# Attention and gated MLP in split fp32: P times V of a head pair in one group instead of two, and narrower score matmuls

## The chip, the cores and the metric

The kernel runs on one core of a Trainium2 chip. The metric is device time in microseconds; three runs of the kernel before gave a median of 1383.16 us (1382.53 to 1386.95).

## The reference

Block-causal attention over 8 batches, 8 heads, 576 positions of 64 dimensions, and then a two-layer MLP with a rational activation:

```python
scores = scale * np.matmul(q, k.transpose(0, 1, 3, 2))
mask = block_i >= block_j                 # blocks of 64 positions
scores = np.where(mask, scores, -1000000000.0)
attn = softmax(scores)                    # with the row maximum taken off, 1e-9 added to the sum
x = concat_heads(np.matmul(attn, v))      # (4608, 512)
h = x @ w_in                              # (4608, 2048)
g = (a0 + a1*h + a2*h**2 + a3*h**3) / (1 + |b0|*|h| + |b1|*h**2 + 1e-6)
out = g @ w_out                           # (4608, 512)
```

## The kernel before

**Number format.** Every operand of a large matmul is held as a high and a low part of type F32R, whose sum is the fp32 value. A product is three matmuls: high by low, high by high, low by high. Transposes on TensorE (PE) are in plain fp32.

**Attention.** The 64 heads are handled as 32 pairs, one pair after the other (NV = 32; four pairs to a batch). The 576 query rows of a pair are five tiles t: 64 rows, then four times 128 (NQ, starting at Q0). Tile t needs the first NK[t] keys: 64, 192, 320, 448, 576. For a tile and one head j, `scores` issues two matmuls (L432, L433) that give S for 128 rows and at least 256 columns, and, but for t = 0, a third (L436) that adds the mask to the last 64 columns; VectorE (DVE) takes the row maximum (L437). `expo` does the exponential on ScalarE (ACT, L449) and the normalization on GpSimd (POOL, L458, L462). `transp` turns P of both heads into blocks of 128 keys by up to 128 queries (L481); each group of blocks in one PSUM bank is copied by ACT to the high part (L486) and subtracted by DVE to the low part (L487). There are 1 + 2t blocks for tile t.

**P times V.** `pv` runs twice per pair. Group 0 follows tile 2 and covers the 320 query columns of tiles 0 to 2: block 0 over 320 columns from the tiles `pt0`, blocks 1 to 4 over 256 columns from `pt1`, whose part that tile 1 doesn't have is zero. Group 1 follows tile 4 and covers the 256 columns of tiles 3 and 4: nine blocks from `pt2`. V stands in `vpad`, two heads side by side; `vprep` fills it for the next pair after group 1. The result (PSUM tile `o`) is split into `x` by ACT (L503) and DVE (L504) and written to a DRAM scratch `xscr`, one DMA for each group (L505).

**MLP.** Its unit of work is 2 x 128 hidden columns by 256 tokens in phase 0 (18 chunks c of 5 units u, the first 10 hidden blocks) and 128 by 512 in phase 1 (the other 6 blocks). `first` does 24 matmuls (L207), then ACT, POOL and DVE compute the activation (L214 to L240), and `second` does 12 matmuls of 512 columns (L257). Phase 0 is threaded through the attention from the fifth pair on; what is left of it and phase 1 follow after the attention. While the attention runs, `split_weights` also splits the weights (L122 to L149).

**What sets the order.** The program is written out as a list of steps: the item of tile t and head j of a pair is one step, ten steps to a pair; `transp` of a tile comes nine steps after its scores, `pv` one step after that. A scheduler then reorders each engine's instructions by a simulated timeline, so neighbouring work moves when an instruction changes. Each engine takes its instructions strictly in that order; SP issues the DMAs.

**Buffers.** Scores, transposed P and `o` share a ring of five PSUM banks (`ps_a`, tag "a"). `pt0`, `pt1`, `pt2` and `vpad` exist once, so the next pair may overwrite a block only after P times V has read it.

Of the kernel before, what the change touches and what calls it, by code (L numbers as in the profile page):

```python
# [9 lines left out]
F32 = mybir.dt.float32  # L10
# [51 lines left out]
def attn_ffn_kernel(  # L62
# [11 lines left out]
    nc = tc.nc  # L74
# [231 lines left out]
    NK = [64, 192, 320, 448, 576]  # L306

    wpool = ctx.enter_context(tc.tile_pool(name="wA", bufs=1))
    with ExitStack() as actx:
# [5 lines left out]
        pt0 = [apers.tile([128, 1, 320], F32R, name=f"pt0{x}") for x in "hl"]  # L315
        pt1 = [apers.tile([128, 4, 256], F32R, name=f"pt1{x}") for x in "hl"]
        pt2 = [apers.tile([128, 9, 256], F32R, name=f"pt2{x}") for x in "hl"]

        vpad = [apers.tile([128, 128 + 4 * 192], F32R, name=f"vp{x}") for x in "hl"]
        for x in pt1:  # L320
            nc.vector.memset(x[:, 2:4, 0:128].bitcast(F32), 0.0)
        for x in pt2:
            nc.vector.memset(x[:, 7:9, 0:128].bitcast(F32), 0.0)
# [90 lines left out]
        def scores(p, t, j):  # L414
# [13 lines left out]
            for i, (c0, w) in enumerate(pieces(t)):  # L428
                ww = max(w, 256)
                ps = ps_a.tile([128, 512], F32, name=f"s{p}_{t}_{j}_{i}", tag="a")  # L430
                last = t > 0 and c0 + w == NK[t]
                nc.tensor.matmul(ps[:, :ww], lhsT=kq[:, 0, qs], rhs=kq[:, 1, c0:c0 + ww], start=True, stop=False)  # L432
                nc.tensor.matmul(ps[:, :ww], lhsT=kq[:, 0, qs], rhs=kq[:, 2, c0:c0 + ww],  # L433
                                 start=False, stop=not last)
                if last:
                    nc.tensor.matmul(ps[:, w - 64:w], lhsT=mrow, rhs=mcol, start=False, stop=True)  # L436
                nc.vector.reduce_max(out=nm[:nq, j, i:i + 1], in_=ps[:nq, :w], axis=AX.X, negate=True)  # L437
                banks.append(ps)
# [27 lines left out]
        def transp(p, t):  # L466
# [3 lines left out]
            groups = {1: [1], 3: [1, 2], 5: [1, 4], 7: [4, 3], 9: [3, 3, 3]}[nb]  # L470
            blk = 0
            for gi, gn in enumerate(groups):
                ps = bank(p, f"t{p}_{t}_{gi}").rearrange("p (c t) -> p c t", c=4)
                for i in range(gn):
# [3 lines left out]
                    else:  # L478
# [3 lines left out]
                (hi, lo), b0, c0 = ((pt2, blk, Q0[t] - 320) if t > 2 else (pt0, 0, Q0[t]) if blk == 0 else  # L482
                                    (pt1, blk - 1, Q0[t] - 64))
                dh = hi[:, b0:b0 + gn, c0:c0 + nq]
                dl = lo[:, b0:b0 + gn, c0:c0 + nq]
# [4 lines left out]
        def pv(p, g):  # L490
            b, hp = divmod(visits[p][0], NPAIR)
            vh, vl = vpad
            nb, w = ((5, 320), (9, 256))[g]
            o = ps_a.tile([128, 512], F32, name=f"o{p}_{g}", tag="a")
            for x in range(nb):
                s0 = 64 if (g == 0 and x > 0) else 0
                hi, lo = ((y[:, x] for y in pt2) if g else (y[:, 0] for y in pt0) if x == 0 else
                          (y[:, x - 1] for y in pt1))
                for i, (vv, pp) in enumerate(((vh, lo), (vh, hi), (vl, hi))):
                    nc.tensor.matmul(o[:, s0:w], lhsT=vblock(vv, x), rhs=pp,  # L500
                                     start=(x == 0 and i == 0), stop=(x == nb - 1 and i == 2))
            xs = att.tile([128, 2, 320], F32R, name=f"x{p}_{g}", tag="xs", bufs=1)
            nc.scalar.copy(out=xs[:, 0, :w], in_=o[:, :w])  # L503
            nc.vector.tensor_tensor(out=xs[:, 1, :w], in0=o[:, :w], in1=xs[:, 0, :w].bitcast(F32), op=ALU.subtract)  # L504
            nc.sync.dma_start(out=xscr[b][:, hp, :, g * 320:g * 320 + w], in_=xs[:, :, :w].bitcast(F32))  # L505
# [7 lines left out]
        def attn_steps():  # L513
# [8 lines left out]
            for k in range(len(items) + ALAG2 + ALAG3 + 8):  # L522
# [3 lines left out]
                if k < len(items):  # L526
# [9 lines left out]
                    if j == 1:  # L536
                        lag = min(ALAG3, nxt[k] - 1)
                        at(k + lag, transp, p, t)
                        if t in (2, 4):
                            at(k + lag + 1, pv, p, t // 4)  # L540
                            if t == ts[-1] and p + 1 < NV:
# [90 lines left out]
```

## Time and profile before

| | |
|---|---|
| median of three runs | 1383.16 us |
| the profiled execution, span from first to last instruction | 1379.1 us |
| PE busy | 1278.1 us, 93% of the span |
| DVE, POOL, ACT busy | 1027.2, 958.2, 909.4 us |
| attention ends (last DMA of `x`) | 980.6 us |

The profile page holds no time for the profiled execution but its span; the median of the runs is 4.1 us above that span, and all sums below are differences made against the span. In a timeline row of PE the first number is the start and the second the modelled duration of the matmul, which overlaps the next one; the distance from one start to the next is what a matmul costs in a stream. PEld is the weight load that goes with each matmul.

### The profile page before, as it was taken

To read this page: it belongs to the slowest core of one execution; us is meant where nothing else is said; L and a number is where in the kernel's file an instruction comes from. 1 tells how busy PE (TensorE), PEld (TensorE's weight loads), DVE (VectorE), ACT (ScalarE), POOL (GpSimd) and SP (SyncE) were. 2 spreads that over 40 slices of the span, in tenths; PEclk is the share of its full clock that TensorE was granted. 3 is DMA by queue.
4 is the path that set the end of the run, shared out by engine and by line. 5 is a ranking of instruction groups with operands and counts; after the bars stand their busy time and mean duration, and the time that the engine had idled before them with its cause. 6 is when DMAs were issued, how large, how long until landed. Compare 5 with 4: busy or idle time off the path is not lost.

```text
span 1379.1 us, 24416 instructions
## 1 busy us (share of the span) xinstructions
PE 1278.1 (93%) x8088; PEld 1149.6 (83%) x8088; DVE 1027.2 (74%) x2048; ACT 909.4 (66%) x2250; POOL 958.2 (69%) x1240
## 2 busy tenths in 40 slices
PE   4677899999899979999999999999989999999997
PEld 3667788999888879888998999998979888888885
DVE  5898877787778857887767777776676767676675
ACT  4766767777677756777767777776645655555553
POOL 4889987687678747777767676666556666666654
PEclk9788999999999999999999999999999999999999
DMA  9778556666556655665654555652632233333332
GB/s 216 198 196 238 146 150 166 168 166 181 148 145 150 164 151 132 165 166 153 157 140 123 154 134 122 160 127 65 213 141 77 77 123 123 122 123 123 122 113 86
DMA packets 216925, 200.84 MB, mean 146 GB/s; under 512 B 129504, under 2 KB 184800, under 8 KB 216800
## 3 DMA queue, kind: packets, MB, share of 16 engines
q1 hardware_dynamic: 216736, 199.28, 53.6%
q8 instruction: 65, 1.06, 0.3%
q14 instruction: 60, 0.49, 0.1%
q0 software_dynamic: 64, 0.00, 0.0%
HBM read 98.57 MB, written 44.04 MB: 103 GB/s over the span
## 4 chain that ended last, share of the span: by engine, by line
PE 69%; DVE 9%; POOL 9%; DMA 5%; ACT 3%; issue 3%; SPq 1%; POOLq 0%; DVEq 0%; ACTq 0%
PE h L207 25%; PE o L257 24%; PE o L500 8%; PE t L481 4%; PE s L432 3%; PE s L433 2%; PE tp L366 2%; POOL gl L240 1%; POOL p L462 1%; DMA x<-xscr 1%; POOL u L217 1%; DVE v L231 1%; DVE nm L437 1%; POOL v L216 1%; DMA xscr<-x 1%
## 5 line engine op out<-in xcount | busy, mean ns | idle before, releaser
L207 PE MATMUL h<-x,wih 128*128 128x256 f32 (+1 forms) x1872 | 415.7, 313 | 9.0 <-DMA x<-xscr 7.9
L207 PEld LDWEIGHTS h<-x,wih 128*128 128x128 f32 x1872 | 309.7, 191 | 29.1 <-issue 6.6
L207 PE MATMUL h<-x,wil 128*128 128x256 f32 (+1 forms) x936 | 290.7, 311 | 0.0
L240 POOL TENSOR_TENSOR gl<-s,gh 128x512 fp32r<-128x512 f32 x144 | 188.8, 1313 | 106.4 <-ACT gh L239 103.0
L257 PE MATMUL o<-woh,gl 128*128 128x512 f32 x576 | 232.2, 403 | 12.1 <-POOL gl L240 10.6
L257 PE MATMUL o<-wol,gh 128*128 128x512 f32 x576 | 227.7, 396 | 0.0
L257 PE MATMUL o<-woh,gh 128*128 128x512 f32 x576 | 227.7, 395 | 0.0
L437 DVE TENSOR_REDUCE nm<-s 128x1 f32<-128x288 f32 (+4 forms) x384 | 161.7, 427 | 78.4 <-PE s L436 45.2
L449 ACT ACTIVATE p<-s,nm 128x288 f32<-128x288 f32 (+4 forms) x384 | 184.9, 485 | 48.3 <-DVE nm L437 35.0
L217 POOL TENSOR_TENSOR u<-v,u 128x512 f32<-128x512 f32 x144 | 189.6, 1317 | 9.8
L216 POOL TENSOR_SCALAR v<-u,bab 128x512 f32<-128x512 f32 x144 | 118.9, 826 | 98.1 <-ACT u L214 94.6
L207 PEld LDWEIGHTS h<-x,wil 128*128 128x128 f32 x936 | 178.7, 191 | 8.7
L462 POOL TENSOR_SCALAR p<-p,rc 128x128 f32<-128x128 f32 (+3 forms) x256 | 164.8, 655 | 29.6 <-DVE rc L457 27.7
L218 DVE TENSOR_TENSOR s<-s,h 128x512 f32<-128x512 f32 x144 | 98.5, 684 | 100.1 <-ACT s L215 99.4
L432 PE MATMUL s<-kq 128*128 128x256 f32 (+3 forms) x384 | 137.3, 360 | 24.3 <-DMA kq<-hl 8.9
L224 ACT ACTIVATE v<-u,qcb 128x512 f32<-128x512 f32 x144 | 104.6, 726 | 69.6 <-POOL u L217 68.9
L214 ACT ACTIVATE u<-h 128x512 f32<-128x512 f32 x144 | 85.9, 596 | 94.2 <-PE h L207 90.1
L239 ACT CAST gh<-s 128x512 fp32r<-128x512 f32 x144 | 89.2, 623 | 82.1 <-DVE s L232 81.5
L257 PEld LDWEIGHTS o<-woh,gl 128*128 128x128 f32 x576 | 109.2, 190 | 35.5 <-POOL gl L240 14.3
L257 PEld LDWEIGHTS o<-wol,gh 128*128 128x128 f32 x576 | 109.1, 189 | 22.2
L257 PEld LDWEIGHTS o<-woh,gh 128*128 128x128 f32 x576 | 109.3, 190 | 18.9
L433 PE MATMUL s<-kq 128*128 128x256 f32 (+3 forms) x384 | 120.1, 315 | 0.0
(105 smaller groups left out, 3043.5 us busy)
## 6 DMA issues: line engine op xcount, KB each, us to landing
kq<-hl SPq DMA_DIRECT2D x64, 432.0 KB, 4.3
kq<-hl SPq DMA_DIRECT2D x64, 288.0 KB, 5.3
x<-xscr SPq DMA_DIRECT2D x56, 256.0 KB, 4.2
xscr<-x SPq DMA_DIRECT2D x32, 320.0 KB, 4.7
qr<-in_q_dram SPq DMA_DIRECT2D x64, 144.0 KB, 2.9
kr<-in_k_dram SPq DMA_DIRECT2D x64, 144.0 KB, 3.0
kq<-hl SPq DMA_DIRECT2D x64, 144.0 KB, 4.8
pscr<-os SPq DMA_DIRECT2D x18, 512.0 KB, 2.9
```

The costliest lines, as they stand in the source:

```text
L207: nc.tensor.matmul(h[:, j, :], lhsT=w[:, dc, fs], rhs=xs[dc][:, hl, :], start=(dc == 0 and i == 0), stop=(dc == 3 and i == 2))
L216: nc.gpsimd.tensor_scalar(out=vt, in0=ut, scalar1=b1, scalar2=b0, op0=ALU.mult, op1=ALU.add)
L217: nc.gpsimd.tensor_tensor(out=ut, in0=vt, in1=ut, op=ALU.mult)
L224: nc.scalar.activation(out=vt, in_=ut, func=AF.Ln, bias=qcb)
L240: nc.gpsimd.tensor_tensor(out=gl.rearrange("p j t -> p (j t)"), in0=st, in1=gh.rearrange("p j t -> p (j t)").bitcast(F32), op=ALU.subtract)
L257: nc.tensor.matmul(self.o[m], lhsT=g[:, j, ms], rhs=w[:, f, :], start=(u == 0 and j == 0 and i == 0), stop=(u == nu - 1 and j == NBU[ph] - ...
L432: nc.tensor.matmul(ps[:, :ww], lhsT=kq[:, 0, qs], rhs=kq[:, 1, c0:c0 + ww], start=True, stop=False)
L433: nc.tensor.matmul(ps[:, :ww], lhsT=kq[:, 0, qs], rhs=kq[:, 2, c0:c0 + ww], start=False, stop=not last)
L437: nc.vector.reduce_max(out=nm[:nq, j, i:i + 1], in_=ps[:nq, :w], axis=AX.X, negate=True)
L449: nc.scalar.activation(out=pt[:nq, j, c0:c0 + w], in_=banks[i][:nq, :w], func=AF.Exp, bias=nm[:nq, j, 0:1], scale=1.0, accum_out=sm[:nq, j ...
L462: nc.gpsimd.tensor_scalar(out=pt[:nq, jj, 64:n], in0=pt[:nq, jj, 64:n], scalar1=rc[:nq, jj:jj + 1], scalar2=1.0, op0=ALU.mult, op1=ALU.mult)
L500: nc.tensor.matmul(o[:, s0:w], lhsT=vblock(vv, x), rhs=pp, start=(x == 0 and i == 0), stop=(x == nb - 1 and i == 2))
```

## The change

P times V becomes one group per pair, issued after tile 4, over 64 columns (tile 0) and 512 columns (tiles 1 to 4). All transposed P of a pair lives in one tile pair `ptr` of 30 blocks of 128 columns: block x of tile t in slot 7(t-1)+x, tile 0 in the first half of slot 12. With that spacing, block x of the tiles c0+1 to 4 is one strided operand (slots 7 apart), and a matmul covers 512, 384, 256 or 128 columns, just those tiles that have the block. The zeroing of `pt1` and `pt2` goes away. The result is split into free slots of the same tile (second half of slot 12, and slots 3 to 6) and written with four DMAs instead of two. Transposes of tile 1 fill one bank instead of two, those of tile 2 go as 3 + 2 instead of 1 + 4. The score matmuls of the tiles 0 and 1 are 64 and 192 columns wide instead of 256.

```diff
-                ww = max(w, 256)
+                ww = w
...
-            groups = {1: [1], 3: [1, 2], 5: [1, 4], 7: [4, 3], 9: [3, 3, 3]}[nb]
+            groups = {1: [1], 3: [3], 5: [3, 2], 7: [4, 3], 9: [3, 3, 3]}[nb]
...
+                b0 = PT0 if t == 0 else 7 * (t - 1) + blk
+                dh, dl = (y[:, b0:b0 + gn, 0:nq] for y in ptr)
...
-        def pv(p, g):
+        def pv(p):
...
+            for i, (vv, pp) in enumerate(((vh, pl), (vh, ph), (vl, ph))):
+                nc.tensor.matmul(o0[:, 0:64], lhsT=vblock(vv, 0), rhs=pp[:, PT0, 0:64],
+                                 start=i == 0, stop=i == 2)
...
+            for x in range(9):
+                c0 = max(0, (x - 1) // 2)
+                for i, (vv, pp) in enumerate(((vh, pl), (vh, ph), (vl, ph))):
+                    nc.tensor.matmul(o1b[:, c0:4, :], lhsT=vblock(vv, x), rhs=pp[:, 7 * c0 + x:22 + x:7, :],
+                                     start=(x == 0 and i == 0), stop=(x == 8 and i == 2))
+            xh0, xl0 = (y[:, PT0, 64:128] for y in ptr)
+            xh1, xl1 = (y[:, 3:7, :].rearrange("p c t -> p (c t)") for y in ptr)
+            for o, xh, xl, q0, w in ((o0, xh0, xl0, 0, 64), (o1, xh1, xl1, 64, 512)):
+                nc.scalar.copy(out=xh, in_=o[:, :w])
+                nc.vector.tensor_tensor(out=xl, in0=o[:, :w], in1=xh.bitcast(F32), op=ALU.subtract)
+                for k, y in enumerate((xh, xl)):
+                    nc.sync.dma_start(out=xscr[b][:, hp, k, q0:q0 + w], in_=y.bitcast(F32))
...
-                        if t in (2, 4):
-                            at(k + lag + 1, pv, p, t // 4)
-                            if t == ts[-1] and p + 1 < NV:
+                        if t == 4:
+                            at(k + lag + 1, pv, p)
+                            if p + 1 < NV:
                                 at(k + lag + 1, vprep, p + 1)
```

Three places in the program show what moves. In the rows, `o12` is P times V of pair 12, `s13_4_0_1` the scores of pair 13, tile 4, head 0, second half, `tp14` the transposes of Q and K of pair 14, `h0_4_0` the first layer of MLP phase 0, chunk 4, unit 0. Line numbers of the changed kernel differ by a few.

PE before, at group 0 of pair 12, half a pair ahead of group 1:

```order
L436 MATMUL s13_2_0_0_5016<-mcol_102,mrow_101 128x64
L500 MATMUL o12_0_5059<-pt0l_129,vph_134 128x320 [waits DVE_49,PE_49,Activation_49]
L500 MATMUL o12_0_5059<-pt0h_128,vph_134 128x320
L500 MATMUL o12_0_5059<-pt0h_128,vpl_135 128x320 [waits Pool_49]
L366 MATMUL tp14_1_0_5079<-ident_96,kr14_4859 128x96 [waits DMAHW6_49,DMAHW5_49]
L366 MATMUL tp14_1_0_5079<-ident_96,kr14_4859 128x96 x2
L366 MATMUL tp14_1_1_5085<-ident_96,kr14_4859 128x96 [waits PE_49]
L366 MATMUL tp14_1_1_5085<-ident_96,kr14_4859 128x96 x2
L500 MATMUL o12_0_5059<-pt1l_131,vph_134 128x256 [waits DVE_49]
```

PE in the changed kernel, where all of pair 12 stands behind tile 4:

```order
L431 MATMUL s13_4_0_1_5017<-mcol_102,mrow_101 128x64
L489 MATMUL o12_0_5023<-ptrl_129,vph_130 128x64 [waits DVE_49,PE_49]
L489 MATMUL o12_0_5023<-ptrh_128,vph_130 128x64
L489 MATMUL o12_0_5023<-ptrh_128,vpl_131 128x64
L207 MATMUL h0_4_0_5448<-x0_4_0_5279,wih0_134 128x256 [waits DVE_49]
```

The two waits for half-finished P in the middle of the pair are gone; unit 0 of chunk 4 now begins inside pair 12's P times V, while before it stood ahead of pair 11's, as the next rows show.

PE before, around the start of chunk 4 (`o0_3_1` is the second layer of chunk 3; some rows further comes `o11_1`):

```order
L257 MATMUL o0_3_1_5445<-woh0_144,gl0_3_3_5671 128x512
L257 MATMUL o0_3_1_5445<-woh0_144,gh0_3_3_5670 128x512
L257 MATMUL o0_3_1_5445<-wol0_145,gh0_3_3_5670 128x512
L207 MATMUL h0_4_0_5674<-x0_4_0_5485,wih0_142 128x256 [waits DVE_49]
L207 MATMUL h0_4_0_5674<-x0_4_0_5485,wih0_142 128x256
```

PE in the changed kernel at the end of pair 12's P times V:

```order
L496 MATMUL o12_1_5027<-ptrl_129,vph_130 128x128
L496 MATMUL o12_1_5027<-ptrh_128,vph_130 128x128
L496 MATMUL o12_1_5027<-ptrh_128,vpl_131 128x128
L427 MATMUL s13_4_1_0_5073<-kq13_1_4433 128x288 [waits PE_49]
L428 MATMUL s13_4_1_0_5073<-kq13_1_4433 128x288
```

So the MLP falls behind the attention: in the order before, 15.1 chunks of first-layer matmuls stand ahead of the last P times V, in the changed one 14.0.

ACT in the changed kernel at the same place (`vph` is V of pair 13, `t13_0_0` its first transposed P, `u0_4_0` the activation of unit 0):

```order
L388 CAST vph_130<-vr13_4271 64x64 [waits DMAHW6_49,PE_49]
L388 CAST vph_130<-vr13_4271 64x64 [waits DMAHW0_49]
L388 CAST vph_130<-vr13_4271 128x4x64 [waits PE_49]
L388 CAST vph_130<-vr13_4271 128x4x64 [waits DMAHW1_49,PE_49]
L501 CAST ptrh_128<-o12_1_5027 128x512 [waits PE_49]
L479 CAST ptrh_128<-t13_0_0_5104 128x64 [waits PE_49]
L214 ACTIVATE u0_4_0_5473<-h0_4_0_5448 128x512 [waits PE_49]
```

Behind the copy of `o12_1`, which waits for the whole P times V, stand the next pair's first copy into the same tile and the activation of the MLP unit.

More of the change, by code (lines that the diff above doesn't have):

```diff
@@ L306, in attn_ffn_kernel @@
     NK = [64, 192, 320, 448, 576]
+    PT0 = 12
     wpool = ctx.enter_context(tc.tile_pool(name="wA", bufs=1))
@@ L312, in attn_ffn_kernel @@
         apers = actx.enter_context(tc.tile_pool(name="apers", bufs=1))
-        pt0 = [apers.tile([128, 1, 320], F32R, name=f"pt0{x}") for x in "hl"]
-        pt1 = [apers.tile([128, 4, 256], F32R, name=f"pt1{x}") for x in "hl"]
-        pt2 = [apers.tile([128, 9, 256], F32R, name=f"pt2{x}") for x in "hl"]
+        ptr = [apers.tile([128, 30, 128], F32R, name=f"ptr{x}") for x in "hl"]
         vpad = [apers.tile([128, 128 + 4 * 192], F32R, name=f"vp{x}") for x in "hl"]
[L320 to L323, printed above, removed]
         for x in vpad:
@@ L481, in transp @@
                     nc.tensor.transpose(ps[:, i, :nq], src, ident[:nq, :nq])
[L482 to L485, printed above, removed]
+                b0 = PT0 if t == 0 else 7 * (t - 1) + blk
+                dh, dl = (y[:, b0:b0 + gn, 0:nq] for y in ptr)
                 nc.scalar.copy(out=dh, in_=ps[:, :gn, :nq])
@@ L488, in transp @@
                 blk += gn
-        def pv(p, g):
+        def pv(p):
             b, hp = divmod(visits[p][0], NPAIR)
             vh, vl = vpad
[L493 to L505, printed above, removed]
+            ph, pl = ptr
+            o0 = ps_a.tile([128, 512], F32, name=f"o{p}_0", tag="a")
+            for i, (vv, pp) in enumerate(((vh, pl), (vh, ph), (vl, ph))):
+                nc.tensor.matmul(o0[:, 0:64], lhsT=vblock(vv, 0), rhs=pp[:, PT0, 0:64],
+                                 start=i == 0, stop=i == 2)
+            o1 = ps_a.tile([128, 512], F32, name=f"o{p}_1", tag="a")
+            o1b = o1.rearrange("p (c t) -> p c t", c=4)
+            for x in range(9):
[10 more added lines that the diff above has]
+                    nc.sync.dma_start(out=xscr[b][:, hp, k, q0:q0 + w], in_=y.bitcast(F32))
```

## The prediction

> **What bounds the kernel now.** I read the page first, then three stretches of the execution, then the chain of work that ended last, then what TensorE waited for, and last single starts of matmuls. From the page:
>
> ```profile
> span 1379.1 us, 24416 instructions
> PE 1278.1 (93%) x8088; PEld 1149.6 (83%) x8088; DVE 1027.2 (74%) x2048; ACT 909.4 (66%) x2250; POOL 958.2 (69%) x1240
> ...
> PE   4677899999899979999999999999989999999997
> DVE  5898877787778857887767777776676767676675
> ...
> PE 69%; DVE 9%; POOL 9%; DMA 5%; ACT 3%; issue 3%; SPq 1%; POOLq 0%; DVEq 0%; ACTq 0%
> PE h L207 25%; PE o L257 24%; PE o L500 8%; PE t L481 4%; PE s L432 3%; PE s L433 2%; PE tp L366 2%; POOL gl L240 1%; POOL p L462 1%; DMA x<-xscr 1%; POOL u L217 1%; DVE v L231 1%; DVE nm L437 1%; POOL v L216 1%; DMA xscr<-x 1%
> ```
>
> PE is busy throughout but for the first slices, and carries 69% of the chain. An average over stages with different limits doesn't price a change, so I cut the span where the sixth pair ends (about 200 us) and where the attention ends (about 985 us):
>
> ```profile
> core 0: us, PE busy (x) PEld busy (x) DVE busy (x) ACT busy (x) POOL busy (x), PEclk, DMA share, GB/s
> 0.00:200.00 200.00, 145.47 (x905) 131.30 (x906) 162.92 (x373) 133.90 (x385) 163.00 (x218) 0.87 0.76 193
> 200.00:985.00 785.00, 754.41 (x5382) 700.12 (x5381) 594.56 (x1297) 559.15 (x1517) 559.78 (x817) 1.00 0.58 146
> 985.00:1379.00 394.00, 378.25 (x1806) 318.19 (x1805) 269.70 (x379) 216.35 (x349) 235.42 (x205) 0.98 0.36 122
> ```
>
> Three stages with two limits: up to 200 us DVE and POOL (163 of 200 us each) are busier than PE (145); from 200 to 985 PE is busy 754 of 785 us, 96%, at full clock; after the attention again 96%. So a microsecond of PE work is worth about a microsecond in the later stages and less in the first. What PE still waits for between 200 and 1000 us:
>
> ```profile
> PE h L207 <- DMA x<-xscr: 7.9, 3, 3.0
> PE o L500 <- DVE pt0l L487: 6.0, 4, 2.1
> PE o L257 <- POOL gl L240: 5.8, 7, 1.4
> ```
>
> The second row is P times V, group 0, standing right behind the transposes whose low part it needs.
>
> **What a matmul costs by its width.** Durations overlap, so I take distances between starts, from the order of time on PE (start, modelled duration, count at the end):
>
> ```profile
> 602.78 0.40 PE L257 MATMUL o<-woh,gl 128*128 128x512 f32 x1
> ...
> 605.08 0.27 PE L481 MATMUL t<-ident,pk 128*128 128x128 f32 x1
> 605.19 0.38 PE L481 MATMUL t<-ident,p 128*128 128x128 f32 x2
> ...
> 611.27 0.31 PE L500 MATMUL o<-pt0h,vph 128*128 128x320 f32 x1
> 611.42 0.31 PE L500 MATMUL o<-pt0h,vpl 128*128 128x320 f32 x1
> ...
> 614.15 0.28 PE L500 MATMUL o<-pt1l,vph 128*128 128x256 f32 x1
> ...
> 614.75 0.28 PE L500 MATMUL o<-pt1h,vpl 128*128 128x256 f32 x1
> ...
> 615.16 0.19 PE L436 MATMUL s<-mcol,mrow 128*128 128x64 f32 x1
> 615.19 0.30 PE L481 MATMUL t<-ident,pk 128*128 128x128 f32 x1
> 615.34 0.38 PE L481 MATMUL t<-ident,p 128*128 128x128 f32 x2
> ```
>
> Ten matmuls of 512 columns stand between 602.78 and 605.08: 0.230 us each. Five of 256 columns between 614.15 and 614.75: 0.120 each. 320 columns: 0.15. The slope is (0.230 - 0.120) / 256 = 0.43 ns per column, so 384 columns are put at 0.175. Below 256 the trace has only the mask of 64 columns, and there the weights of the next matmul decide:
>
> ```profile
> 605.65 0.19 PE L436 MATMUL s<-mcol,mrow 128*128 128x64 f32 x1
> 605.65 0.19 PEld L257 LDWEIGHTS o<-woh,gh 128*128 128x128 f32 x1
> 605.68 0.47 PE L257 MATMUL o<-woh,gh 128*128 128x512 f32 x1
> ...
> 605.76 0.19 PEld L257 LDWEIGHTS o<-wol,gh 128*128 128x128 f32 x1
> ```
>
> The load for the next matmul begins with the mask (605.65), and the load after it only 0.11 us later, when the next matmul has really started: the mask costs 0.11 us although 64 columns at 0.43 ns are 0.03. So a matmul of 64, 128 or 192 columns is put at 0.11, hardly less than one of 256. The Trainium skill ("TensorE: Matmul & The Clock Gate", Back-to-back issue gap) gives about 81 ns per matmul of 128 columns in a stream of weight loads and matmuls. By its figure the 544 narrow matmuls below would cost 0.03 us less each, some 16 us in all; the row above disagrees for these operands, and I stay with 0.11.
>
> **The change, part by part.**
>
> *P times V on PE.* Removed: 3 matmuls of 320 and 39 of 256 columns per pair, over 32 pairs 96 x 0.15 + 1248 x 0.120 = 164.2 us. Added: per pair 3 of 64, 9 of 512, 6 of 384, 6 of 256 and 6 of 128: 288 x 0.230 + 192 x 0.175 + 192 x 0.120 + 288 x 0.11 = 154.5 us. Gain 9.7 us. The zero blocks were a sixth of the columns, but what takes their place is partly narrow, and narrow ones pay for weights.
>
> *Scores of 64 and 192 columns.* 256 matmuls from 0.120 to 0.11: 2.6 us. PE work falls by 12.3 us in all.
>
> *Groups of transposes and the split of the result.* The durations on DVE:
>
> ```profile
> L487 DVE TENSOR_TENSOR pt2l<-t,pt2h 128x384 fp32r<-128x384 f32 x128 | 68.8, 547 | 3.9 <-ACT pt2h L486 3.7
> ...
> L487 DVE TENSOR_TENSOR pt1l<-t,pt1h 128x512 fp32r<-128x512 f32 x32 | 21.8, 681 | 0.3 <-ACT pt1h L486 0.2
> L487 DVE TENSOR_TENSOR pt0l<-t,pt0h 128x128 fp32r<-128x128 f32 x64 | 18.1, 283 | 3.9 <-ACT pt0h L486 3.6
> L504 DVE TENSOR_TENSOR x<-o,x 128x320 fp32r<-128x320 f32 x32 | 15.5, 483 | 2.9 <-ACT x L503 2.9
> L487 DVE TENSOR_TENSOR pt1l<-t,pt1h 128x256 fp32r<-128x256 f32 x32 | 13.3, 415 | 2.0 <-ACT pt1h L486 1.8
> L504 DVE TENSOR_TENSOR x<-o,x 128x256 fp32r<-128x256 f32 x32 | 13.2, 412 | 3.7 <-ACT x L503 3.6
> L487 DVE TENSOR_TENSOR pt0l<-t,pt0h 128x64 fp32r<-128x64 f32 x32 | 6.7, 211 | 0.2 <-ACT pt0h L486 0.2
> ```
>
> Tile 1: 283 + 415 becomes 547, 0.15 us less per pair; tile 2: 283 + 681 against 547 + 415, nothing; the result: 483 + 412 against 211 + 681, nothing. That is 4.8 us of DVE over the kernel, and about as much on ACT. From 200 us on PE's work hides it; in the first stage, six pairs, it is 0.9 us.
>
> *DMAs.* Four writes of the result per pair instead of two, 64 issues more on SP:
>
> ```profile
> L505 SPq DMA_DIRECT2D xscr<-x x64: 359/388/2122, 46.2 to 980.6; - x64
> ```
>
> At the median of 388 ns that is 25 us of a queue that spends far longer waiting than issuing; the loads of Q, K and V for later pairs stand behind them, pairs ahead of need. Bytes and packets stay the same (512 per pair). Between nothing and 0.8 us per pair on the chain, I take nothing.
>
> *The waits in the middle of a pair.* Group 0 goes, and with it the wait for `pt0l` (6.0 us in the row above). The one P times V that remains waits for tile 4's low part as group 1 did. Between 0 and 7 us, I take 4, since a part of it will appear at the new place.
>
> *What the order moves.* The MLP falls behind: ahead of the last P times V stand 129 first-layer (256 columns) and 72 second-layer matmuls (512 columns) fewer, 129 x 0.120 + 72 x 0.230 = 32.1 us of PE work, and they come after the attention. Ahead of the sixth pair's P times V it is 45 and 25, 11.1 us. So PE work changes by stage: the first loses 11.1 + 12.3 x 6/32 = 13.4 us; the second 12.3 + 32.1 - 13.4 = 31.0 us; the last gains 32.1 us.
>
> **The sum.** First stage: PE isn't the limit, but the moved MLP units take their DVE, POOL and ACT work along. Between 0 and 13.4 us, I take half, 6.7. Second stage: 31.0 (0.96 of it, 29.8, at the least). Last stage: 32.1 at 96% busy is 33.4. So 6.7 + 31.0 - 33.4 + 4 = 8.3 us less: span 1371, and with the 4.1 us by which the median of the runs lies above the span, 1375 us against 1383.2. The lower end takes all: 13.4 + 31.0 - 32.1 + 7, 19 us, 1364; allowing for the narrow score matmuls ahead of a transpose, whose weights load faster (615.16 to 615.34, less 0.11 for the transpose, leaves 0.07 for the mask), 1362.
>
> **The rivals.**
>
> *The gain drowns in the shift.* If the first stage gives nothing, the second 29.8 and the waits nothing, the shift costs more than the rest saves: 33.4 - 29.8 = 3.6 us, 1387. For it speaks that DVE and POOL bound the first stage; against it, that moving a unit out relieves them too. No measurable change, within 0.3% (4.1 us), is all from 1379 to 1387.
>
> *Slower: one tile of P, read once at the end.* Group 0 read its blocks half a pair before the next pair wrote them. Now the next pair's first copies stand on ACT behind the copy of the whole result, with an MLP activation behind them, and PE starts 30 matmuls that need the last tile. If PE then stands as long as a wait for `pt0l` (6.0 / 4 = 1.5 us), it takes 8.3 / 1.5, six pairs, to eat the gain; at 13 of 26 pairs it is 19.5 us, 1394. Against it: P times V before waited for tile 4 in the same way and its rows show no large wait.
>
> *Narrow or strided operands stream slower.* If a column below 256 cost twice (0.86 ns), 192 columns would cost 0.175 and 128 columns 0.12: 128 x 0.065 + 192 x 0.01 = 10.2 us, 1385. Four times is excluded for 64 columns by the 0.07 us of the mask, which would be 0.11. For the rows of 512 columns in four pieces no row exists: each piece costs between nothing and a matmul's fixed part, 0.120 - 256 x 0.00043 = 0.010 us, which is 1248 further pieces, 12.5 us, 1387. The Trainium skill ("Advanced Engine Details and Errata", SBUF Cachelines) says that reads are at full rate while they stay in a line of 16 bytes; each piece here is 512 bytes, so by it the pieces are free. No run here shows that.
>
> **Chances.** My forecast, faster than 1379: 0.57. The drowned gain: 0.20. One tile: 0.14. Narrow or strided: 0.09, half of it no change and half slower. So faster 0.57, same 0.25, slower 0.18. For 8 in 10 the range reaches from 1362 into the slower case, to 1391; the forecast's own is 1364 to 1379.
>
> **What would show it.** P times V should show 960 matmuls with starts 0.23 (512), 0.12 (256) and 0.11 (128 and 64) apart, and score matmuls 0.11; the attention should end near 940 us instead of 981 and the stretch after it last some 430 us instead of 398. Wrong is the forecast if PE waits in front of P times V grow past 10 us, if the copies into the tile wait for it, if the narrow matmuls are further apart than those of 256, or if PE's share from 200 us to the attention's end falls below 94%.

## The result and the profile after

The changed kernel takes 1395.6 us against 1386.5 us for the kernel before, run beside it: 1.0077 times as long, 95% interval 1.0055 to 1.0098. It is 0.8% slower, with the whole interval above 1, and outside the range of the prediction. The profiled execution has a span of 1391.8 us, 12.7 us more than before. From the page of the changed kernel:

```profile
span 1391.8 us, 23765 instructions
PE 1275.2 (92%) x7704; PEld 1132.3 (81%) x7704; DVE 1020.0 (73%) x2012; ACT 907.3 (65%) x2218; POOL 953.8 (69%) x1240
...
PE   4676789999999899999999999999999999999997
PEclk9677899999999999999999999999999999999999
...
PE 62%; DVE 14%; DMA 8%; POOL 8%; ACT 4%; issue 3%; SPq 2%; POOLq 0%; DVEq 0%; ACTq 0%
```

384 matmuls fewer, PE 3 us less busy, and yet a longer span: the work went down and the time did not follow. The span less PE's busy time is the time in which PE stands idle: 101.0 us before, 116.6 after. PE's share of the chain fell from 69% to 62%; DVE (9% to 14%) and DMA (5% to 8%) took it over, so PE waits longer for results and loads.

The stretches now have to be cut where each kernel's own stages end: at the write of the sixth pair's result (202.4 us before, 204.1 after) and at the last write of the attention (980.6 and 970.8). First the kernel before, then the changed one:

```profile
core 0: us, PE busy (x) PEld busy (x) DVE busy (x) ACT busy (x) POOL busy (x), PEclk, DMA share, GB/s
0.00:202.40 202.40, 147.87 (x917) 133.36 (x918) 165.32 (x380) 133.90 (x385) 164.29 (x219) 0.87 0.75 192
202.40:980.60 778.20, 747.61 (x5343) 694.15 (x5342) 590.72 (x1289) 556.61 (x1512) 556.43 (x814) 1.00 0.58 146
980.60:1379.10 398.50, 382.65 (x1832) 322.10 (x1831) 271.14 (x382) 218.89 (x353) 237.48 (x207) 0.98 0.36 121
```

```profile
0.00:204.10 204.10, 137.86 (x764) 122.20 (x765) 155.83 (x356) 131.45 (x375) 152.70 (x214) 0.82 0.73 183
204.10:970.80 766.70, 730.66 (x4942) 665.80 (x4941) 574.75 (x1252) 542.75 (x1467) 550.23 (x806) 0.99 0.60 151
970.80:1391.80 421.00, 406.72 (x2001) 344.29 (x1999) 289.43 (x404) 233.08 (x378) 250.86 (x220) 0.99 0.34 113
```

A busy PE is not a PE at work: a modelled duration counts as busy, and at half clock it counts double. So I also sum the matmuls of each stage at the distances between their starts that were measured (0.227 us for 512 columns, the median over each trace, 0.120 for 256, 0.11 below, 0.06 for 64 columns ahead of a transpose), and call that the matmul work. It is an estimate: the sums are good to a few us, their differences to about one.

| stage | work before | work after | change | change of time |
|---|---|---|---|---|
| to the sixth pair | 111.7 | 95.4 | -16.3 | +1.7 |
| to the attention's end | 722.2 | 696.2 | -26.0 | -11.5 |
| the rest | 377.7 | 404.0 | +26.3 | +22.5 |
| sum | 1211.7 | 1195.6 | -16.1 | +12.7 |

The 26.0 us of work that left the second stage shortened it by 11.5 us, and the 16.3 that left the first shortened it by nothing; what came back after the attention was paid almost in full. Two things fill the gap. PE's idle time grew by 15.6 us: 11.7 more in the first stage, 5.4 more in the second, 1.6 less in the last. And PE's clock stood at half for 92 us instead of 71: 20 us more in the first stage, 7 more in the second, 6 less in the last. As work takes twice as long then, half of such time is lost at most. In the second stage that makes 5.4 and at most 3.4 of the 14.5 us that are missing; the other 6 show in no row.

What PE waits for, in the kernel before and then in the changed one:

```profile
PE s L432 <- DMA kq<-hl: 8.9, 3, 4.7
...
PE o L500 <- DVE pt0l L487: 7.5, 6, 2.1
...
PE tp L366 <- DMA kr<-in_k_dram: 4.3, 4, 1.5
...
PE o L500 <- DVE pt1l L487: 2.4, 2, 2.0
...
PE o L500 <- DVE pt2l L487: 1.7, 1, 1.7
```

```profile
PE tp L361 <- DMA kr<-in_k_dram: 15.1, 10, 3.2
PE o L496 <- DVE ptrl L480: 9.7, 5, 4.6
PE s L427 <- DMA kq<-hl: 9.0, 3, 5.7
...
PE s L427 <- DVE ptrl L480: 4.6, 9, 0.8
PE t L476 <- DVE ptrl L480: 4.6, 9, 0.9
```

The first row is the transposes of K that wait for K's load. In the kernel before it was 4.3 us in all; no other wait grew as much. The second is P times V waiting for the last low part of P; the three rows of `o` before sum to 11.6 us.

The matmuls themselves run as forecast. Rows of PE's timeline in the changed kernel, one P times V (column 1 is the start):

```profile
589.58 0.39 PE L496 MATMUL o<-ptrh,vph 128*128 128x512 f32 x1
589.81 0.40 PE L496 MATMUL o<-ptrh,vpl 128*128 128x512 f32 x1
...
591.43 0.34 PE L496 MATMUL o<-ptrl,vph 128*128 128x384 f32 x1
591.61 0.34 PE L496 MATMUL o<-ptrh,vph 128*128 128x384 f32 x1
...
592.50 0.28 PE L496 MATMUL o<-ptrl,vph 128*128 128x256 f32 x1
592.62 0.28 PE L496 MATMUL o<-ptrh,vph 128*128 128x256 f32 x1
...
593.38 0.27 PE L496 MATMUL o<-ptrh,vpl 128*128 128x128 f32 x1
593.49 0.27 PE L496 MATMUL o<-ptrl,vph 128*128 128x128 f32 x1
```

0.23 us for 512 columns in four pieces, 0.18 for 384, 0.12 for 256 in two pieces, 0.11 for 128. Strided operands and narrow matmuls take no longer than forecast, so the loss is not there.

### The profile page after: what moved, and what is told of

The parts are those of the page before. It is cut to its first block, busy times and chain, and to the rows that moved or that the text cites. A ratio compares the mean times of both kernels' runs of the same rounds, so it can differ in the third digit from the quotient of the medians.

```text
span 1391.8 us, 23765 instructions
## 1 busy us (share of the span) xinstructions
PE 1275.2 (92%) x7704; PEld 1132.3 (81%) x7704; DVE 1020.0 (73%) x2012; ACT 907.3 (65%) x2218; POOL 953.8 (69%) x1240
## 4 chain that ended last, share of the span: by engine, by line
PE 62%; DVE 14%; DMA 8%; POOL 8%; ACT 4%; issue 3%; SPq 2%; POOLq 0%; DVEq 0%; ACTq 0%
PE h L207 23%; PE o L257 21%; PE o L496 8%; PE t L476 3%; PE s L427 2%; DVE nm L432 2%; DMA x<-xscr 2%; PE s L428 2%; DVE ptrl L480 2%; POOL u L217 2%; PE tp L361 1%; POOL gl L240 1%; DMA kr<-in_k_dram 1%; DVE s L232 1%; ACT p L444 1%
## 5 line engine op out<-in xcount | busy, mean ns | idle before, releaser
L216 POOL TENSOR_SCALAR v<-u,bab 128x512 f32<-128x512 f32 x144 | 117.5, 816 | 94.3 <-ACT u L214 91.7
L427 PE MATMUL s<-kq 128*128 128x288 f32 (+4 forms) x384 | 134.5, 353 | 33.0 <-DMA kq<-hl 9.0
L480 DVE TENSOR_TENSOR ptrl<-t,ptrh 128x384 fp32r<-128x384 f32 (+3 forms) x288 | 143.4, 509 | 11.5 <-ACT ptrh L479 10.9
L479 ACT CAST ptrh<-t 128x384 fp32r<-128x384 f32 (+3 forms) x288 | 123.2, 456 | 31.1 <-PE t L476 29.4
```

The lines of the kernel that those rows point to most:

```text
L216: nc.gpsimd.tensor_scalar(out=vt, in0=ut, scalar1=b1, scalar2=b0, op0=ALU.mult, op1=ALU.add)
L479: nc.scalar.copy(out=dh, in_=ps[:, :gn, :nq])
L480: nc.vector.tensor_tensor(out=dl, in0=ps[:, :gn, :nq], in1=dh.bitcast(F32), op=ALU.subtract)
```

## The experiments

All ratios are against the kernel before, run beside the experiment, with 95% intervals. Two theories recur in the expectations. One says that the merged P times V took away work that stood in the middle of a pair and covered other waits. The other says that every order the scheduler puts out has a time of its own, scattered by about a per cent, whatever edit made it. Others concern one wait (K's load), and whether work that is taken out of a fixed order shortens the time.

For the last question, and to part a width from the order that it leads to, some kernels change the width of matmuls after the scheduler has put out its order. Nothing else changes then, neither the order of any engine nor the semaphores that it waits for. The added lines are given here in words:

```diff
     with _tile.TileContext(nc, schedule_with_timeline_sim=True) as tc:
         attn_ffn_kernel(tc, *args)
+    for each score matmul s<p>_<t>_<j>_0 <- kq with t = 0 or 1:
+        output and moving operand get (64, 192)[t] columns
```

**Width or order: four kernels.** e2 is the kernel before with `ww = w` alone: narrow scores, and the order that the scheduler makes of them. e5 is the kernel before with the widths cut after scheduling (narrow scores, old order). e6 is e2 with the widths put back to 256 after scheduling (wide scores, new order).

```diff
-                ww = max(w, 256)
+                ww = w
```

> The kernel before with score matmuls of 64 and 192 columns alone. Theory A: ratio 0.996 to 0.999 (2.6 to 5 us of matmul work less, P times V untouched). Rival B (narrow scores cost the time): 1.005 to 1.010. Rival C (order scatters): anywhere from 0.993 to 1.012.

> The kernel before, scheduled with score matmuls of 256 columns, whose 256 matmuls of the tiles 0 and 1 are then cut to 64 and 192 columns without touching the order. Theory S (the narrow matmuls themselves cost no more, the reordered program does): ratio 0.995 to 1.001, TensorE work 3 to 5 us less, waits as in the kernel before. Rival N (narrow matmuls are slow where they stand, whatever the order): 1.012 to 1.020, as the kernel with narrow scores alone (1.018).

> The reverse: scheduled with scores of 64 and 192 columns, whose matmuls are then widened to 256 columns without touching the order. Theory S: ratio 1.016 to 1.024, as slow as the narrow kernel of the same order or 2 to 5 us more. Rival N: 0.998 to 1.003.

| | order of before | order of e2 |
|---|---|---|
| scores 256 wide | 1 | e6: 1407.6 us, 1.0182 (1.0158 to 1.0207) |
| scores 64 and 192 | e5: 1380.5 us, 0.9987 (0.9972 to 1.0002) | e2: 1406.6 us, 1.0182 (1.0163 to 1.0201) |

The columns of the table differ by 1.8 to 2.0%, its rows by no more than 0.13%. So e5 and e6 came out as theory S said, while all three expectations for e2 failed, that of scatter too (at most 1.012). An edit that takes a little work off PE costs 25 us because the scheduler answers it with another order. Where e2 loses part of it is seen at the end of the attention. The longest of PE's waits in e2, and the same stretch in e2 and then in before:

```profile
PE h L207 <- DMA x<-xscr: 19.1, 7, 9.0
```

```profile
990.00:1010.00 20.00, 9.54 (x56) 8.01 (x54) 3.58 (x5) 3.92 (x7) 3.31 (x3) 0.86 1.03 364
```

```profile
990.00:1010.00 20.00, 18.05 (x109) 15.63 (x108) 17.54 (x18) 11.40 (x18) 13.81 (x12) 1.00 1.05 400
```

PE stands for half of 20 us, because the last pair's result has to go to DRAM and come back before the MLP can go on, and e2's order has nothing else there; the single wait is 9.0 us. Before has 18 us of work in the same place. This explains at most 9 of e2's 25 us. Over the whole of e2, PE's idle time is 117.5 us instead of 101.0, and it stands at half clock for 92 us instead of 71.

**The changed kernel with wide scores.** e1 undoes that part of the change before scheduling.

```diff
-                ww = w
+                ww = max(w, 256)
```

> The changed kernel with score matmuls of at least 256 columns again; P times V stays in one group. Theory A (the mid-pair P times V was cover: without it TensorE idles between the transposes and scores of the pair's middle): the narrow scores are not to blame, 2.6 us more matmul work, ratio to before 1.008 to 1.012, TensorE idle in the K transposes still near 11 us from 200 us to the attention's end. Rival B (the narrow scores let the scheduler push the MLP back, which costs the time): ratio 0.998 to 1.002 and the MLP no longer a chunk behind. Rival C (the scheduler's order scatters by some 10 us whatever is edited): anywhere from 0.993 to 1.012.

1388.3 us, 1.0047 (1.0032 to 1.0063): with more work than the changed kernel, not more time, and probably less (the two intervals overlap a little). Theory A and rival B both missed; only the wide bounds of scatter hold it. Its waits for K's load are 5.1 us instead of 15.1.

**One group or two.** e3 is the changed kernel (one tile, strided operands, narrow scores, new groups of transposes) with P times V in two groups at the old places. e4 is the changed kernel with the old groups of transposes.

```diff
-        def pv(p):
+        def pv(p, g):
...
-                        if t == 4:
-                            at(k + lag + 1, pv, p)
+                        if t in (2, 4):
+                            at(k + lag + 1, pv, p, t // 4)
```

> The changed kernel's tile, strided operands, narrow scores and groups of transposes, but P times V in two groups at their old places: tiles 0 to 2 after tile 2, tiles 3 and 4 after tile 4 (matmuls of 64, 128 and 256 columns, six DMAs per pair). Matmul work is some 3 us above the kernel before's P times V and 3 to 5 us below its scores. Theory A (the place of group 0 decides): ratio 0.996 to 1.003, waits of TensorE for the K load back at 2 to 4 us. Rival D (the one tile, its strided operands or the narrow matmuls decide): 1.007 or more.

```diff
-            groups = {1: [1], 3: [3], 5: [3, 2], 7: [4, 3], 9: [3, 3, 3]}[nb]
+            groups = {1: [1], 3: [1, 2], 5: [1, 4], 7: [4, 3], 9: [3, 3, 3]}[nb]
```

> The changed kernel with the transposes of tiles 1 and 2 in banks of 1 + 2 and 1 + 4 blocks as before. Theory A: the grouping is worth 0.15 us of VectorE and ScalarE per pair, hidden: ratio 1.006 to 1.011, as the changed kernel. Rival E (the tile 1 bank of three blocks holds a bank longer and so delays the scores): 0.998 to 1.003. Rival C (order scatters): 0.993 to 1.015.

e3: 1386.0 us, 1.0019 (1.0006 to 1.0032). e4: 1405.6 us, 1.0162 (1.0143 to 1.0181). Putting the group in the middle of the pair back recovers most of the loss, as theory A forecast. But e4, which leaves the merged P times V and only shares out the same copies in another way, costs 0.85% more than the changed kernel, outside every expectation (the widest ended at 1.015). Its largest wait:

```profile
PE tp L361 <- DMA kr<-in_k_dram: 28.8, 13, 4.7
```

That wait is 13.7 us more than in the changed kernel, but PE's idle time is only 2.3 us more (118.9 against 116.6): other waits became shorter. What e4 adds is time at half clock, 122 us instead of 92, with a mean granted clock of 0.957 instead of 0.967.

The load of K is a matter of the order. The raw Q and K of a pair share one buffer (`raw`, one copy), so K's load is issued only when Q's transposes have read theirs, and it lands 2.4 to 5.7 us later (median 3.1, changed kernel); whatever the order puts between Q's and K's transposes covers it. Worked out from each kernel's order with the measured distances, the work missing there below 4.4 us (a bound that I set), summed over the pairs from the fourth on, and the waits of the trace:

| | before | after | e1 | e2 | e3 | e4 |
|---|---|---|---|---|---|---|
| missing cover, us | 12.3 | 21.1 | 14.2 | 9.0 | 5.8 | 37.3 |
| wait for K's load, us | 4.3 | 15.1 | 5.1 | 3.9 | 2.1 | 28.8 |

The two go together in all six: they explain the wait. What the wait is worth in time is another question, as e4 shows. A second copy of the buffer would have tested it directly; that wasn't tried.

**K's transposes a step later.** e7 (changed kernel) and e8 (kernel before) move them from step 5 to step 6 of a pair.

```diff
-OFFS = {5:(0,3,5)}
+OFFS = {5:(0,3,6)}
```

> The changed kernel with the transposes of K one step later (three steps instead of two behind those of Q, whose buffer the K load waits for). By the order, matmul work short of 4.4 us between the two falls from 21 us to 8 us. Theory K (the wait for the K load is the largest part of what was lost): TensorE's wait for the K load falls from 15 us to below 6 and the ratio from 1.008 to 0.996 to 1.001. Rival (the wait only moves on, to the scores' banks and operands): the K wait falls but the ratio stays at 1.004 or more.

> The kernel before with the same step. Short work falls from 12 us to 1 us. Theory K: ratio 0.990 to 0.997, K and Q load waits of TensorE near zero after the start. Rival (the wait moves on): 0.999 to 1.006.

e7: 1386.7 us, 1.0035 (1.0017 to 1.0052), 0.4% less than the changed kernel. e8: 1384.8 us, 1.0018 (1.0000 to 1.0037), no gain. Theory K had forecast more in both, and missed. In e7 two rows tell why:

```profile
PE s L427 <- DMA kq<-hl: 20.0, 6, 6.9
...
PE tp L361 <- DMA kr<-in_k_dram: 2.8, 3, 1.5
```

The wait for K's load falls from 15.1 to 2.8 us, but the transfer of the split K to the two heads (`kq`), which comes next, is now late: 20.0 instead of 9.0 us. Together the two fall by 1.3 us only: the wait moved on, as the rival said. PE's idle time fell by 9 us all the same (116.6 to 107.6), in other rows. So K's load is the largest wait that the new order brought, but how much of the lost time it cost is not shown.

**Less work in a fixed order.** In e9 (order of before) and e10 (order of after) the P times V matmuls beyond the first three of each result are cut to 64 columns after scheduling; the columns beyond the cut are left out of the result.

> The kernel before in its own order, with the matmuls of P times V behind the first three of each group cut to 64 columns after scheduling (so a part of P times V is left out): 13 us of matmul work less, about the size of what the change removes. Theory F (at a fixed order matmul work counts nearly in full): ratio 0.989 to 0.994. Rival W (waits set the pace, removed work turns into idle time): 0.997 to 1.001.

> The changed kernel in its own order, with the matmuls of the 512-column group behind the first three cut to 64 columns after scheduling (a part of P times V is left out): 37 us of matmul work less. Theory F: from 1.008 to between 0.981 and 0.989. Rival W: 0.995 or more.

| | matmul work | time | ratio | granted clock of the profiled execution |
|---|---|---|---|---|
| before | 1211.7 | | 1 | 0.974 |
| e9 | 1198.3 | 1395.4 | 1.0076 (1.0051 to 1.0101) | 0.950 |
| after | 1195.6 | 1395.6 | 1.0077 (1.0055 to 1.0098) | 0.967 |
| e10 | 1158.8 | 1390.1 | 1.0055 (1.0036 to 1.0074) | 0.940 |

13 us less work made e9 slower, and 37 us less gave e10 hardly anything, with the order untouched. Theory F missed in both, and rival W in e9 too. The last column points to a reason. Here are two neighbouring stretches of e9, each as long as the steps in which its clock changes, and rows from the first of them:

```profile
813.96:817.37 3.41, 3.41 (x31) 3.34 (x30) 3.04 (x7) 3.14 (x11) 3.26 (x5) 1.00 0.81 165
817.37:820.78 3.41, 3.41 (x16) 3.35 (x16) 1.53 (x7) 3.03 (x11) 3.13 (x6) 0.51 0.66 170
```

```profile
814.49 0.28 PE L500 MATMUL o<-pt2l,vph 128*128 128x64 f32 x1
814.60 0.28 PE L500 MATMUL o<-pt2h,vph 128*128 128x64 f32 x1
814.71 0.28 PE L500 MATMUL o<-pt2h,vpl 128*128 128x64 f32 x1
```

PE doesn't idle for a moment in the first stretch, yet the clock is halved in the second, and 16 instead of 31 matmuls start. What is special is the 64 columns: a matmul starts every 0.11 us but streams for 64 x 0.42 ns = 0.027 us (0.42 ns is the slope from 0.120 us for 256 columns to 0.227 for 512). All matmuls of the stretch together stream for 0.34 of it (transposes counted twice, a choice that parts the cases best). I counted this for every such step of 3.4 us in the traces of before, after, e9 and e10: ahead of a halving it was never above 0.43; where the full clock stayed, never below 0.33; between the two either happened. With the busy share there is no such line, as the rows show. So the theory for the next runs: the clock follows the share of time in which columns stream.

**The same work with more columns.** e13 and e14 repeat e9 and e10 with 192 columns instead of 64, which take the same 0.11 us. e15 is the changed kernel with its 64-column scores at 192. Like e9 and e10, e13 and e14 leave a part of P times V out of the result.

> The order of before with the P times V matmuls beyond the first three of each group cut to 192 columns instead of the 64 of e9 (part of P times V is left out). A matmul of 64 and one of 192 columns take the same 0.11 us, so the matmul work is that of e9, 13 us less than before; only the share of time in which columns stream differs, 192 x 0.42 ns = 0.080 of 0.11 us instead of 0.027. Clock theory (the clock is halved after a window of 3.4 us in which columns stream for less than about 0.38 of the time, however busy PE is): granted clock back at 0.965 to 0.975 instead of 0.950, half clock for some 75 to 100 us instead of 141, and 10 to 25 us less than e9, 1370 to 1383 us, ratio 0.990 to 1.000. Rival (work taken out of a fixed order is worth nothing because other engines or waits fill the room): clock no matter, time like e9, ratio 1.005 to 1.010.

> The order of after with its P times V matmuls of 256 to 512 columns beyond the first three cut to 192 columns (two pieces of 96) instead of the 64 of e10 (part of P times V is left out); those of 128 stay. Each takes 0.11 us as in e10, so the matmul work is that of e10, about 37 us less than after. Clock theory: granted clock 0.960 to 0.970 instead of 0.940 and 15 to 30 us less than e10, 1360 to 1375 us, ratio 0.983 to 0.995. Rival (work taken out of a fixed order is worth nothing): like e10, ratio 1.003 to 1.008.

> The order of after, unchanged, with the 128 score matmuls of 64 columns widened to 192 after the order was made. Both widths take 0.11 us, so the matmul work stays; only the streamed columns rise, for 8 matmuls per pair by 0.05 us each. Clock theory: some windows of the first stage cross the bound, clock 0.967 to 0.975, 0 to 8 us less than after, 1387 to 1396 us. Rival (the clock loss of after comes from its waits, not from narrow matmuls): no change, 1393 to 1397, ratio 1.006 to 1.010.

| | matmul work | time | ratio | granted clock |
|---|---|---|---|---|
| e13 (as e9, 192 columns) | 1199.0 | 1381.3 | 0.9972 (0.9959 to 0.9986) | 0.967 |
| e14 (as e10, 192 columns) | 1158.8 | 1377.2 | 0.9948 (0.9933 to 0.9963) | 0.956 |
| e15 (after, scores 192) | 1196.5 | 1393.6 | 1.0068 (1.0054 to 1.0082) | 0.963 |

Each P times V of 192 columns against one of 64, at equal work and in the same order, is 1.0 to 1.1% faster. A burst of P times V in e13, at 803.07 to 806.33 us, and the step's length behind it, where the clock stays:

```profile
803.10:806.50 3.40, 3.40 (x32) 3.40 (x32) 3.21 (x8) 3.14 (x10) 3.25 (x6) 1.00 0.64 130
806.50:809.90 3.40, 3.40 (x28) 3.27 (x28) 1.98 (x6) 3.40 (x13) 3.40 (x5) 1.00 0.68 154
```

Two things follow. The clock theory holds in the main: e13 came out as it said, while e14 went its way but less far (clock 0.956 where at least 0.960 was expected, 1377.2 us where at most 1375 was); the rival, with ratios of 1.003 and more, is out. The same count of steps over e13, e14 and e15, from which the theory was not made, parts without overlap: 42 halvings, none after a share above 0.38, and 1052 steps in which the full clock stayed, none after a share below 0.38.

And a fairer price of work in a fixed order can be read: e13 gains 0.28% or 3.9 us for 12.7 us of work, e14 against the changed kernel 1.29% or 18 us for 37. So a microsecond of PE work out of this kernel brought 0.3 to 0.5 us (0.15 to 0.6 by the intervals). Some clock is still lost in both; if it is allowed for at the rate of e9 and e13 (14 us for 0.020 of mean granted clock over all runs), the price is about 0.5 to 0.6, an estimate, and still well below 1. And e15, whose interval overlaps that of the changed kernel and whose clock did not rise, says that the few narrow scores are not what costs the changed kernel its clock: there the rival was right. The falls of its clock all come after steps in which PE stood for over a third of the time: there it follows the waits.

**Orders that keep the gain.** The last five runs make an order in one way and the widths in another. "Planned" means scheduled as if the scores had 256 columns, and cut afterwards. e11 is e3, planned, with K's transposes at step 7; e12 the changed kernel, planned, with step 6; e16 the changed kernel, planned, step 5 as it was; e17 is e12 with scores of 192 columns in both tiles; e18 is e12's treatment of the kernel before, with its two groups and four tiles.

> A version to beat both: one tile of transposed P, P times V in two groups, scheduled with wide scores and narrowed afterwards, transposes of K two steps later (work short of 4.4 us between Q and K: 2 us). Theory K and S together: ratio 0.988 to 0.997. Rival (orders scatter, no rule of mine orders them): 0.998 to 1.010.

> The changed kernel scheduled with wide scores, narrowed afterwards, transposes of K one step later: matmul work as the changed kernel, work short between Q and K 8 us instead of 21. Theory K and S together: ratio 0.992 to 1.001. Rival (orders scatter): 1.002 to 1.012.

> One of the two edits of e12 alone: after, with its order made as if the scores of tiles 0 and 1 had 256 columns (the order of e1), and the matmuls cut to 64 and 192 afterwards; K's transposes stay where after has them. If the plan is the edit that counts: 1371 to 1378 us, ratio 0.992 to 0.997. If the later K transposes count: like e1 less at most 3.4 us of work, 1384 to 1389, ratio 1.001 to 1.005. Each order has a time of its own within a per cent (the theory that orders scatter): anything from 1372 to 1390.

> e12 with the 128 score matmuls of 64 columns widened to 192 after the order was made, as in e15. The matmul work is that of e12 (0.11 us for either width). By e15 (1393.6 against 1395.6 in after) the streamed columns are too few to matter: 1369 to 1375 us, ratio 0.990 to 0.994. If the clock of e12's first stage hangs on them: 3 to 6 us less than e12, 0.986 to 0.990.

> What e12 did, without the merged P times V: before's two groups and its four tiles, the order made with K's transposes one step later and wide scores, the matmuls of tiles 0 and 1 cut to 64 and 192 columns afterwards. If e12's gain is the treatment and not the merged P times V: 1370 to 1376 us, ratio 0.990 to 0.995. If the merged P times V and the order that goes with it count: e8 (1.0018) with e5's step (-0.0013), 1382 to 1385 us, ratio 0.999 to 1.002.

| | P times V | planned | K's step | time | ratio |
|---|---|---|---|---|---|
| after | one group | no | 5 | 1395.6 | 1.0077 (1.0055 to 1.0098) |
| e7 | one group | no | 6 | 1386.7 | 1.0035 (1.0017 to 1.0052) |
| e16 | one group | yes | 5 | 1387.8 | 1.0034 (1.0020 to 1.0048) |
| e12 | one group | yes | 6 | 1371.8 | 0.9922 (0.9906 to 0.9938) |
| e17 | one group, scores 192 | yes | 6 | 1370.9 | 0.9915 (0.9895 to 0.9936) |
| e11 | two groups | yes | 7 | 1378.9 | 0.9974 (0.9955 to 0.9993) |
| e18 | two groups, before's tiles | yes | 6 | 1384.2 | 1.0020 (1.0003 to 1.0037) |

e12 and e17 beat both kernels, by 10.9 and 10.6 us against the one before; they are one order with two widths, so one finding and not two. The merged P times V is in them, so it doesn't make a kernel slow by itself, and the lost cover of the pair's middle can't be the whole cause. Five orders of the merged kernel were run, and they stand at 1.0162 (e4, with other groups of transposes), 1.0077 (the change), 1.0035 (e7), 1.0034 (e16, whose order is that of e1) and 0.9922 (e12). e12's two edits bring 0.4% each alone and 1.55% together, so they don't add up, as orders that scatter wouldn't. Without the merge the same treatment gives nothing (e18); but that is one order against one, and doesn't show that the merge brings the gain. Of the expectations, e12 came at the lower end of theories K and S, e16 where the later transposes were held to count, e17 where the columns were held too few to matter, e18 where the merge and its order were held to count, and e11 between its two ranges.

Two lines of e12's page, its first two stretches, and the row of the DMAs that write its results (their last start is the attention's end):

```profile
span 1373.6 us, 23786 instructions
PE 1275.7 (93%) x7704; PEld 1136.0 (83%) x7704; DVE 1018.2 (74%) x2012; ACT 904.1 (66%) x2218; POOL 956.5 (70%) x1240
```

```profile
0.00:200.00 200.00, 141.89 (x778) 125.17 (x778) 150.58 (x359) 131.31 (x377) 154.44 (x217) 0.82 0.76 189
200.00:985.00 785.00, 755.47 (x5106) 691.47 (x5104) 594.86 (x1273) 555.60 (x1489) 563.76 (x817) 0.99 0.61 157
```

```profile
L504 SPq DMA_DIRECT2D xscr<-ptrl x64: 319/448/1950, 56.5 to 965.1; - x64
```

Its attention ends at 965.1 us instead of 970.8, though its order puts more of the MLP ahead of that: by the measured distances 806.0 us of matmul work are done by then, against 791.6 in the changed kernel, out of almost the same sum (1197.0 and 1195.6 us). PE is as busy as in the changed kernel (1275.7 and 1275.2 us) and as long at half clock (94 and 92 us), but idles for 97.9 us instead of 116.6. These 18.7 us less account for the 18.2 us between the two spans. That is what the order is worth: the same matmuls, with other work in the holes. The waits for K's load and for its split make 6 of them (24.1 us in the changed kernel, 18.1 in e12); the others are spread over many short rows.

## Why the prediction was wrong, step by step

*The prices of the matmuls: right.* 0.23, 0.18, 0.12 and 0.11 us, as taken. The matmul work fell by 16.1 us instead of 12.3. The rule of the Trainium skill that I weighed ("TensorE: Matmul & The Clock Gate", Back-to-back issue gap, 81 ns for 128 columns) is not met: 0.11 us for these operands. The one on strided reads ("Advanced Engine Details and Errata", SBUF Cachelines) agrees: four pieces of 512 bytes run at the 0.23 us of 512 columns in one piece. The recorded text has two slips that change nothing: the zero blocks were a seventh of the columns, not a sixth, and the further pieces are 1440, which would have made that rival 1389 us instead of 1387.

*"A microsecond of PE work is worth about a microsecond in the later stages": the step that failed first.* I read it from PE busy for 96% of the second stage. In a fixed order 0.3 to 0.5 us was measured (e13, e14), and the second stage gave 11.5 us for 26.0 (forecast 31.0, and 4 for the waits). Forecast and result lie 21 us apart: the second stage missed by 23.5, the first by 8.4, and the last came out 10.9 better. A busy share is no proof of a bound: with less work PE idled for 5.4 us more in the second stage, its clock stood at half for 7 us more, and some 6 us are in no row. That the modelled durations hide these as short waits, in which PE meets a result that isn't ready, is my reading and not shown. The bound that I named for it, PE's share falling below 94%, did not sound: 730.66 of 766.70 us are 95%.

*The first stage, "half, 6.7": wrong in sign.* 16 us of work left it, more than the 13.4 that I took, and it became 1.7 us longer. PE was not its limit, as said. It idled there for 66.2 us instead of 54.5, and its granted clock went from 0.87 down to 0.82: with more holes between the matmuls, the matmuls that remain run slower.

*The shift of the MLP: right in kind, too large.* 26.3 us of work came to the last stage instead of 32.1, and cost 22.5 instead of 33.4. The attention ended at 971 us, not near 940.

*The waits in the middle of a pair, "I take 4": about 1 was found.* `o<-pt0l`, 7.5 us over the whole kernel before, is gone with `o<-pt1l` and `o<-pt2l`, 11.6 us in all, and `o<-ptrl` takes their place with 10.3 (9.7 for the 512 columns, 0.6 for the 64).

*The loads, "pairs ahead of need": wrong for K.* K's load can't be ahead of need, since its buffer is that of Q until Q's transposes are done. The wait for it rose from 4.3 to 15.1 us. A later step took it away (e7, 2.8 us), but most of it came back as the wait for K's split.

*The rivals.* That the gain drowns in the shift comes nearest in kind (1387 forecast), but it priced only the work that moved, not the quality of the new order. The one-tile rival has the nearest number (1394) by luck: P times V waited no longer than before (10.3 us against 11.6), and the copies into the tile waited for transposes (29.4 of the 31.1 us that ACT stood before them), not for P times V. Narrow or strided operands did not stream slower.

*What I left out.* The scheduler makes a new order from each edit, and I took from it only the shift of the MLP. Narrow scores alone move the time by 1.8% through the order and by 0.1% through the work (e2, e5, e6), and the change itself goes from 1.0077 to 0.9922 in another order (e12). The 1.8% are 25 us, three times the gain that I forecast, and a range of -13 to +16 us did not allow for them.

What stays open: why the scheduler's orders differ as they do; which waits make up the changed kernel's loss, and K's load's part in it, since no single edit removed it; whether the merged P times V itself gains anything at an equally good order; and why e12's two edits do more together than alone.

## What to carry to other kernels

When a scheduler makes the order from the instructions, an edit has two effects, and they can be measured apart: keep the order and change the widths, then keep the widths and change the order. Before giving up an edit that saves work but loses time, try it with a few other orders: here the same merged P times V stands at 1.0077 and at 0.9915. Compare the idle time and the time at half clock beside the work: they show where the saved work went. And look which load can't run ahead because its buffer is shared; a new order may take away the work that covers it.

## What the runs showed of the hardware

The granted clock of PE fell to half in steps of 3.4 us, also with PE issuing without a gap, when the matmuls were narrow: 31 matmuls of mostly 64 columns in 3.41 us, streaming for 0.34 of it, were followed by a step at 0.51 (e9), while with 192 columns at the same distance the clock stayed at 1.00 (e13). In the traces of e13, e14 and e15 all 42 halvings came after steps that streamed for at most 0.38, and after all steps that streamed for more the clock stayed. Over the kernel that was 139 us at half clock in e9 against 91 in e13, and 14 us of time. The Trainium skill ("TensorE: Matmul & The Clock Gate", Part 1: The HAM clock gate) has the clock follow PE's activity in a window of 3413 ns and halve it after an idle one; length and factor agree with the rows, but here the window was not idle by any record, only poor in columns. So a matmul of 64 columns that takes the time of one of 192 can be the dearer one, here 1.0% of the kernel's time.
